# One transfer of 128 rows for each output tile, and another order for the attention of batches 1 and 2, in a global-local attention and gated MLP kernel

## The chip, the cores and the metric

The kernel runs on one core of one Trainium2 chip. The metric is the device time of one execution in microseconds; lower is better.

## The reference

There are 8 batches of 8 heads with head dimension 64. Each batch has 32 global tokens and 512 local ones. The kernel computes attention and puts its output through an MLP (8 x 544 = 4352 tokens, 512 wide, 2048 hidden).

```python
s_g = scale * q_g @ concat(k_g, k_l).T             # global queries see everything
out_g = softmax(s_g) @ concat(v_g, v_l)
s_ll = where(|i - j| <= 32, scale * q_l @ k_l.T, -1e9)   # local queries: a band
s_lg = scale * q_l @ k_g.T                               # and all global keys
out_l = softmax(concat(s_lg, s_ll)) @ concat(v_g, v_l)
x = concat(out_g, out_l) per batch, heads side by side   # (4352, 512)
h = x @ w_in
out = (h * sigmoid(1.702 * h)) @ w_out                   # float32
```

## The kernel before

The order of the instructions on every engine is written out by hand: the tile framework is told to keep the program's order. It adds the semaphore waits.

**Attention.** The unit of work is half a batch, four heads, one for each 32 partitions. `Quad` does batch 0, `Wide` all others; in the text `a` and `c` are the two halves of the batch in work, `a2` the first half of the next. Its methods are the steps:

- `Tk`, `Tq` transpose the loaded keys (`rk`) and queries (`rq`) on VectorE into `kT` and `qt`; `kcopy` and `qcopy` lay some of them out a second time; `transpose_g` does the same for the global queries and keys of a batch (`qgT`, `kgT`), and `ext` copies these beside the local ones. Each copy can run on VectorE or on ScalarE (`on_act`).
- `S(rnd)` computes the scores of one of two rounds on TensorE into a pair of PSUM tiles (`spair`, one buffer each), `X(rnd)` the exponentials on ScalarE, `M(rnd)` the product with the band mask, on VectorE or GpSimd.
- `U(unit)` multiplies the exponentials by ones (unit 0, the sums) and by two halves of the values, `Gm` the same for the global queries. `R` turns the sums into factors on VectorE, `XL(h)` scales into `xL`, the MLP's input; `G` does so for the global rows, into `xG`. `UG` and `RXG` are short for runs of these.

**MLP.** For each batch `h_mm` and `h_act` (together `h_step`) compute one of 16 chunks of the hidden layer for 512 tokens: four matmuls into a bank of PSUM, and a gelu on ScalarE into `gT`. The second product of batches 0 and 1 goes by `o_mm`: sixteen parts of four matmuls, four for each of four tiles of 128 tokens (`osteps` and `o_parts` list them), then `o_out` copies a tile to SBUF on ScalarE and stores it. The second product of later batches goes by `Pair`, with seven products in place of eight (sums of `gT` and of `w_out`, `weight_sums`, are made on VectorE beforehand). The rows of global tokens of all batches, number `B`, form a last block of 256 rows in two tiles.

The banks of PSUM for `hp`, `op`, `ov`, `og`, `px` and `py` come from one pool of four in turn. Exponentials and gelu need different tables in ScalarE; the table is loaded when the function changes, and `exp_table` and `gelu_table` force a load early by an activation of one column.

**Order.** TensorE is kept busy by interleaving: the attention of batch 1 runs among the `osteps` of batch 0, that of batch 2 (and the first half of batch 3) among the `o_parts` of batch 1 in `phase_o1`, later ones in `phase_o`. GpSimd's queue issues the loads of queries, keys, values and weights with a cast to bfloat16, in the order in which they stand between GpSimd's own instructions.

**Stores.** Token t of a tile is not a row of the output in order: within a batch, row `16 r + t` is computed in group t, and a tile has four groups of 32 tokens on 32 partitions each. `tile_out` stores one group after the other:

```python
for j in js:
    rows = out[...].rearrange("(r t) m -> t r m", t=16)[4 * tci + j]   # 32 rows of 512
    eng.dma_start(out=rows, in_=ob[32 * j : 32 * j + 32])
```

SP's queue issues nearly all of them; in the last block GpSimd issues one tile, and ScalarE six quarter pieces. `Pair.store` stores a pair of tiles, `quarter` half the columns of a tile.

Of the kernel before, what the change touches and what calls it, by code (L numbers as in the profile page):

```python
# [20 lines left out]
def kernel(  # L21
# [12 lines left out]
    nc = tc.nc  # L34

    B, H, Sl, D = q_l.shape
    Sg = q_g.shape[2]
    S = Sg + Sl
# [36 lines left out]
    def load(b, us=(0, 1), kq=True):  # L75
        if b not in loaded:
            loaded[b] = (ld.tile([128, 2, 16 * D], BF16, name="rk"),
                         ld.tile([128, 2, 16 * D], BF16, name="rq"))
        if kq:
            s = slice(us[0], us[-1] + 1)  # L80
            nc.gpsimd.dma_start(out=loaded[b][1][:, s], in_=qf[b][:, s])
            nc.gpsimd.dma_start(out=loaded[b][0][:, s], in_=kf[b][:, s])
# [5 lines left out]
    def v_view(b, n):  # L88
        return vtiles[b % 2][:, : 8 * n * (D + 2)].rearrange("p (u j c d) -> p u j c d", u=2, j=4, c=n)
# [16 lines left out]
    def copy_vg1():  # L106
        vt = v_view(1, 5).rearrange("p u j c d -> p (u j) c d")
        src = vt[96:128, :, 0:1, :D]
        on_act(vt[96:128, :, 1:2, :D], src)
        on_act(vt[96:128, :, 3:5, :D], src.to_broadcast([32, 8, 2, D]))  # L110

    def on_act(out_, in_):
        nc.scalar.activation(out_, in_, AF.Copy)  # L113
# [49 lines left out]
    for j in range(4):  # L163
        r = (j + 1) % 4
        nc.gpsimd.memset(bd[32 * r : 32 * r + 32, j, :], 1.0)
    for i in range(2):
# [3 lines left out]
        out=step, in_=step, pattern=[[1, 289]], compare_op=ALU.is_ge,  # L170
# [68 lines left out]
    def transpose_g(lo, hi, names="qk"):  # L239
        for name, dst, s in (("q", qgT, rqg), ("k", kgT, rkg)):  # L240
            if name not in names:
                continue
            nc.vector.transpose(dst[:, lo:hi, :32], s[:, lo:hi].bitcast(F32))
# [39 lines left out]
    def spair():  # L283
        return [psS.tile([128, 2, 512], F32, name="s4", tag="s%d" % i) for i in range(2)]
# [326 lines left out]
    def h_mm(i, fc, hp, kcs):  # L611
        for kc in kcs:
            nc.tensor.matmul(hp[:, : width(i)], lhsT=w_in_c[:, fc // 4, kc, fc % 4 // 2, :, fc % 2],  # L613
                             rhs=(xL[i] if i < B else xG)[:, kc, :],
                             start=(kc == 0), stop=(kc == NKC - 1))
# [7 lines left out]
    def gelu_table():  # L623
        gelu(spot[:, 0:1], spot[:, 1:2])

    def exp_table():
        nc.scalar.activation(spot[:, 0:1], spot[:, 1:2], AF.Exp)
# [5 lines left out]
    def h_step(i, fc):  # L633
        if fc == 0:
            gTs[i] = (moe.tile([128, FC, TB], BF16, name="gT") if i < B else
                      early.bitcast(BF16).rearrange("p a b -> p (a b)").rearrange("p (f t) -> p f t", f=FC))
        hp = pbank("hp")
        h_mm(i, fc, hp, range(NKC))
        h_act(i, fc, hp)

    def o_mm(i, st, out=True):
        tci, f4 = divmod(st, 4)
        first = (i, tci) not in ops
        if first:
            ops[i, tci] = pbank("op")
        op = ops[i, tci]
        for fc in range(4 * f4, 4 * f4 + 4):
            nc.tensor.matmul(op, lhsT=gTs[i][:, fc, tci * 128 : tci * 128 + 128],  # L648
                             rhs=w_out_sb[:, fc, :], start=(first and fc == 4 * f4), stop=(fc == FC - 1))
        if f4 == 3 and out:  # L650
            o_out(i, tci, op)
# [42 lines left out]
    class Pair:  # L694
# [51 lines left out]
        def store(self, engs=(nc.sync, nc.sync)):  # L746
            for h in range(2):
                tile_out(self.i, self.tt + h * (width(self.i) // 256),
                         self.ob[:, 2 * h : 2 * h + 2].rearrange("p h m -> p (h m)"), engs[h])

        def quarter(self, h, m, eng, js=range(4)):
            tile_out(self.i, self.tt + h, self.ob[:, 2 * h + m], eng, slice(m * HM, m * HM + HM), js)

    def tile_out(i, tci, ob, eng=nc.sync, cols=slice(0, d_model), js=range(4)):
        for j in js:
            if i < B:
                rows = out[i * S + Sg : (i + 1) * S, cols].rearrange("(r t) m -> t r m", t=16)[4 * tci + j]
            else:
                r = (4 * tci + j) * S
                rows = out[r : r + Sg, cols]  # L760
            eng.dma_start(out=rows, in_=ob[32 * j : 32 * j + 32])  # L761

    obs = {}

    def o_out(i, tci, op):
        if tci % 2 == 0:
            obs[i, tci // 2] = moe.tile([128, 4, HM], F32, name="ob", bufs=3)
        ob = obs[i, tci // 2][:, tci % 2 * 2 : tci % 2 * 2 + 2].rearrange("p h m -> p (h m)")
        nc.scalar.activation(ob, op, AF.Copy)
        tile_out(i, tci, ob)  # L770

    a, c = Quad(0), Quad(1)
# [81 lines left out]
    def osteps(i, *sts):  # L854
        for tci, f4 in sts:
            o_mm(i, 4 * tci + f4)

    nq = {1: (Wide(2), Wide(3)), 2: (Wide(4), Wide(5))}
    a, c = nq[1]
    copy_vg1()  # L860
    transpose_g(2, 4)
    a.Tk(False)
    a.Tq(False)
    a.ext((0, 1, 2), on_act)
    a.kcopy(on_act)
    a.ext((3,), on_act)
    a.qcopy(on_act)
    osteps(0, (0, 1), (0, 0), (1, 1), (1, 0), (2, 1), (2, 0))
    a.S(0)
    a.X(0)  # L870
    c.Tk()
    c.Tq()
    c.ext()
# [2 lines left out]
    a.S(1)  # L876
    a.X(1)
    a.M(1)
    nq[2][0].Tq(False)
    nq[2][0].Tk(False)  # L880
    osteps(0, (0, 3))
    o_mm(0, 7, False)
    c.S(0)
    c.X(0)
    o_out(0, 1, ops[0, 1])
    c.M(0, nc.gpsimd)
    load(2, (1,))
    load_v(2)
    load(3)
    osteps(0, (2, 3), (3, 0))  # L890
    c.S(1)
    c.X(1)
    nq[2][0].kcopy(on_act)
    nq[2][0].qcopy(on_act)
    for unit in range(3):
        a.U(unit)
    a.R()
# [15 lines left out]
    for kcs in ((0, 1), (2,), (3,)):  # L913
        for fc in range(4):
            h_mm(1, fc, hps[fc], kcs)
    transpose_g(4, 6)
    a.G()
    c.G()
    pt = spair()
    for fc in range(4, 8):  # L920
        h_mm(1, fc, bank(pt, (fc - 2) % 4), range(NKC))

    a, c = nq[2]
# [22 lines left out]
    def o_parts(i, *parts):  # L946
        for part in parts:
            o_mm(i, part)

    def loads_after(i):  # L950
        if i + 2 < B:
            load_v(i + 2)
        if i == 1:
            load_g(8, NQ)
        if i + 3 < B:
            load(i + 3)

    def quads_of(n):
        if n < B and n not in nq:
            nq[n] = (Wide(2 * n), Wide(2 * n + 1))  # L960
        return nq.get(n, (None, None))

    def phase_o1():
        a, c = nq[2]
        a2, c2 = quads_of(3)
        a2.T()
        transpose_g(6, 8)
        a2.ext()
        a.X(0)
        a.M(0)  # L970
        loads_after(1)
        o_parts(1, 0, 1, 2, 3, 4)
        a.S(1)
        a.X(1)
        a.M(1)
        o_parts(1, 5, 6)
        c.S(0)
        c.X(0)
        o_parts(1, 7)
        a.UG()  # L980
        a.R()
        c.M(0)
        c.S(1)
        c.X(1)
        a.XL(0)
        a.XL(1)
        c.M(1)
        a.G()
        o_parts(1, 8, 9)
        a2.S(0)  # L990
        a2.X(0)
        o_parts(1, 10, 11)
        a2.M(0)
        a2.S(1)
        a2.X(1)
        gelu_table()
        c.UG()
        c.RXG()
        a2.M(1)
        o_parts(1, 12, 13, 14, 15)  # L1000

    def phase_o(i):
        b = i + 1
# [69 lines left out]
    for i in range(1, B):  # L1073
        if i > 1:
            for fc in range(FC):
# [3 lines left out]
                if i + 1 < B:  # L1079
                    c = nq[i + 1][1]  # L1080
# [23 lines left out]
    def pair_banks(k):  # L1104
        return [psX.tile([128, 512], F32, name="x", tag="x%d" % (2 * (k % 2) + j)) for j in range(2)]
# [3 lines left out]
    for st in range(FC):  # L1109
        h_step(B, st)  # L1110
        if st < len(todo):
            tt, k = todo[st]
            if k == 3:
                p = Pair(B - 1, tt, pair_banks(tt))
            p.mm(k)
            if k == 4:
                p.m3()
                p.z()
            if k == 6:
                p.zm()  # L1120
            if k == 2:
                p.sub()
                p.evict()
            if k == 7:
                p.add()
                p.store((nc.sync, (nc.sync, nc.gpsimd)[tt]))
        if st in (4, 8, 12):
            g_sums(B, st // 2 - 2, st // 2)
        if st == 14:
            g_sums(B, 6, 7)  # L1130
# [3 lines left out]
    p = Pair(B, 0, (x0, x1, y0, y1))  # L1134
# [14 lines left out]
    p.mm(5)  # L1149
    nc.vector.tensor_sub(zz[0], zz[0], x0[:, :HM])  # L1150
    on_act(p.ob[:, 1], x0[:, :HM])
    p.quarter(0, 1, nc.scalar, (0, 1))
    p.quarter(0, 1, nc.sync, (2, 3))
    p.mm(7)
    nc.vector.tensor_add(p.ob[:, 0], zz[0], y0[:, :HM])
    p.quarter(0, 0, nc.scalar)


# [28 lines left out]
```

## Time and profile before

| | |
|---|---|
| median of 3 runs | 290.76 us (290.74 to 291.71) |
| profiled execution | 293.49 us |
| its span | 291.8 us, mean granted clock of TensorE 0.998 |
| busy share: PE, DVE, ACT, POOL | 96%, 69%, 65%, 38% |
| matmuls | 3727 |
| stores issued: SP, ScalarE, GpSimd | 130, 6, 4 |

The profile is of one execution and is the source of all durations; its own time is 2.7 us above the median, and 1.7 us above its span. PE is TensorE's matmuls, PEld its weight loads, DVE is VectorE, ACT ScalarE, POOL GpSimd, SP the sync engine; a q behind the name is the engine's queue of transfers. A row of the timeline gives start and duration in us, engine, line, operation, output and input, and in brackets how long the engine had been idle and what ended that. Lines are those of the kernel before.

### The profile page before, as it was taken

Reading aid. Unit: us, or ns where it says so; the run is one execution under the profiler, and the core shown is the slowest. Engines: PE = TensorE matmul, PEld = TensorE weight load, DVE = VectorE, ACT = ScalarE, POOL = GpSimd, SP = SyncE. Lnnn points to the kernel's source line nnn. Section 1 sums busy time; section 2 is a strip of 40 time slices with the busy share of each in tenths; the row PEclk is TensorE's granted clock in tenths of the full one; section 3 lists DMA queues with packets and bytes.
Section 4 is the critical chain, followed back from the end, with each engine's and each line's share of the span. In section 5 each row is a group of like instructions: output and inputs, shape, how many; then the busy total and the mean of one; then the engine's idle time right before and its main releaser. Section 6 shows DMA issues by size and latency. Waiting matters only on the chain.

```text
span 291.8 us, 8856 instructions
## 1 busy us (share of the span) xinstructions
PE 280.4 (96%) x3727; PEld 179.0 (61%) x3727; DVE 200.5 (69%) x480; ACT 188.4 (65%) x304; POOL 112.2 (38%) x148
## 2 busy tenths in 40 slices
PE   6899989999999999999899999999999999999993
PEld 6444445444554478646685488646874588458882
DVE  7660157974589899579858898679957697263361
ACT  4847588478686775688458784778658761863431
POOL 8893459976217101790049503760071000000020
PEclk9999999999999999999999999999999999999999
DMA  8999999999959901299025942290112002200222
GB/s 202 157 202 208 203 167 159 161 136 164 166 120 128 151 4 39 58 129 156 6 75 81 149 82 66 55 117 5 28 49 72 2 3 74 72 0 2 72 76 73
DMA packets 59480, 28.24 MB, mean 97 GB/s; under 512 B 47600, under 2 KB 49904, under 8 KB 59440
## 3 DMA queue, kind: packets, MB, share of 16 engines
q0 software_dynamic: 51792, 17.83, 54.8%
q1 hardware_dynamic: 7072, 9.12, 11.3%
q10 hardware_dynamic: 576, 0.72, 0.8%
q8 instruction: 29, 0.48, 0.7%
q14 instruction: 11, 0.09, 0.1%
HBM read 36.31 MB, written 8.91 MB: 155 GB/s over the span
## 4 chain that ended last, share of the span: by engine, by line
PE 80%; DMA 10%; POOL 4%; DVE 2%; issue 1%; ACT 1%; DVEq 0%; POOLq 0%
PE hp L613 34%; PE px L719 12%; PE py L719 9%; PE x L719 6%; PE op L648 6%; PE s L558 5%; DMA rq<-in_q_l_dram 5%; PE ov L584 4%; DMA w_out_sb<-in_moe_w_out_dram 3%; DMA v<-in_v_l_dram 2%; PE s L613 1%; POOL mask L225 1%; POOL w_in_sb L259 1%; DVE xL L469 1%; PE og L595 1%
## 5 line engine op out<-in xcount | busy, mean ns | idle before, releaser
L613 PE MATMUL hp<-xL,w_in_sb 128*128 128x512 bf16 x480 | 105.4, 379 | 0.4 <-DVE xL L469 0.4
L613 PEld LDWEIGHTS <-w_in_sb 128*128 128x128 bf16 x576 | 56.0, 98 | 60.4 <-issue 0.7
L618 ACT ACTIVATE gT<-hp 128x512 bf16<-128x512 f32 x120 | 70.4, 596 | 26.4 <-PE hp L613 24.9
L569 ACT ACTIVATE e<-s 128x1016 bf16<-128x1016 f32 (+1 forms) x56 | 53.3, 1004 | 20.3 <-PE s L558 20.1
L574 POOL TENSOR_TENSOR e<-e,mask 128x1760 bf16<-128x1760 bf16 (+1 forms) x9 | 29.6, 3290 | 76.1 <-ACT e L569 76.1
L719 PEld LDWEIGHTS <-gs 128*128 128x128 bf16 x480 | 46.2, 98 | 6.3
L692 DVE TENSOR_TENSOR gs<-gT 128x512 bf16<-128x512 bf16 (+1 forms) x90 | 30.4, 365 | 18.8 <-ACT gT L618 18.7
L98 POOL DMA_DIRECT2D v<-in_v_l_dram x40 | 31.3, 791 | 15.9 <-PE og L595 12.1
L719 PE MATMUL py<-wsum,gs 128*128 128x256 bf16 x240 | 30.3, 273 | 0.0
L648 PE MATMUL op<-w_out_sb,gT 128*128 128x512 bf16 x128 | 29.5, 380 | 0.2 <-DMA w_out_sb<-in_moe_w_out_dram 0.2
L761 POOL DMA_DIRECT2D out_dram<-ob x4 | 2.1, 534 | 61.3 <-ACT early L618 61.3
L574 DVE TENSOR_TENSOR e<-e,mask 128x1712 bf16<-128x1712 bf16 (+1 forms) x19 | 21.0, 1104 | 5.2 <-ACT e L569 5.2
L510 DVE STREAM_TRANSPOSE kT<-rk 128x512 f32<-128x512 f32 x14 | 14.6, 1045 | 9.5 <-DMA rk<-in_k_l_dram 9.5
L648 PEld LDWEIGHTS <-gT 128*128 128x128 bf16 x128 | 11.9, 98 | 14.1 <-issue 0.2
L719 PEld LDWEIGHTS <-gT 128*128 128x128 bf16 x192 | 18.0, 98 | 2.8
L719 PE MATMUL px<-w_out_sb,gT 128*128 128x256 bf16 x160 | 19.2, 273 | 0.0
L719 PE MATMUL px<-w_out_sb,gs 128*128 128x256 bf16 x160 | 19.1, 273 | 0.0
L558 PEld LDWEIGHTS <-kT 32*128 32x128 bf16 x672 | 13.0, 93 | 9.2 <-issue 6.4
L469 DVE TENSOR_TENSOR xL<-ov,rs 128x512 bf16<-128x512 f32 x27 | 17.9, 687 | 0.9 <-PE ov L436 0.4
L689 DVE TENSOR_TENSOR gs<-gT 128x1024 bf16<-128x1024 bf16 (+1 forms) x30 | 17.4, 580 | 0.0
L558 PE MATMUL s<-q,kT 32*128 32x160 bf16 (+1 forms) x448 | 15.4, 246 | 1.5 <-issue 1.0
L113 ACT ACTIVATE ob<-px 128x512 f32<-128x512 f32 x10 | 6.0, 597 | 15.0 <-DVE zz L741 15.0
(149 smaller groups left out, 361.2 us busy)
## 6 DMA issues: line engine op xcount, KB each, us to landing
out_dram<-ob SPq DMA_DIRECT2D x128, 64.0 KB, 1.8
rq<-in_q_l_dram POOLq DMA_DIRECT2D x5, 512.0 KB, 6.4
rk<-in_k_l_dram POOLq DMA_DIRECT2D x5, 512.0 KB, 8.2
v<-in_v_l_dram POOLq DMA_DIRECT2D x24, 96.0 KB, 4.0
w_in_sb<-in_moe_w_in_dram POOLq DMA_DIRECT2D x8, 256.0 KB, 7.7
w_out_sb<-in_moe_w_out_dram POOLq DMA_DIRECT2D x4, 512.0 KB, 10.8
rq<-in_q_l_dram POOLq DMA_DIRECT2D x5, 256.0 KB, 6.2
rk<-in_k_l_dram POOLq DMA_DIRECT2D x5, 256.0 KB, 6.2
```

The lines of the kernel that those rows point to most:

```text
L98: nc.gpsimd.dma_start(out=vt[0:n, hs, c, :D], in_=vs[FIRST[c] : FIRST[c] + n, hs])
L469: nc.vector.tensor_mul(self.x[:, 2 * self.u + h, :], self.st[1 + h], self.st["rs"])
L510: nc.vector.transpose(flat[:, 0:Sl].rearrange("p (r t) -> p t r", t=16), loaded[self.b][0][:, self.u].bitcast(F32))
L558: nc.tensor.matmul(bank(self.ps, j)[:, at : at + n], lhsT=self.k[p, KEYS[c] : KEYS[c] + 128, e], rhs=qs[p, :, :, e], start=(e == 0), stop= ...
L569: nc.scalar.activation(self.E[rnd][:, 2 * i : 2 * i + 2, :n], self.ps[i][:, :, :n], AF.Exp, scale=scale)
L574: eng.tensor_mul(e, e, mask[:, rnd : rnd + 1, :n].to_broadcast([128, 4, n]))
L613: nc.tensor.matmul(hp[:, : width(i)], lhsT=w_in_c[:, fc // 4, kc, fc % 4 // 2, :, fc % 2], rhs=(xL[i] if i < B else xG)[:, kc, :], start=( ...
L618: nc.scalar.activation(out_, in_, AF.Gelu_apprx_sigmoid)
L648: nc.tensor.matmul(op, lhsT=gTs[i][:, fc, tci * 128 : tci * 128 + 128], rhs=w_out_sb[:, fc, :], start=(first and fc == 4 * f4), stop=(fc = ...
L689: nc.vector.tensor_tensor(sums[i][2][:, g, :n], t[:, g, 0, :n], t[:, g, 1, :n], ALU.add)
L692: nc.vector.tensor_tensor(sums[i][k][:, g, : n // 2], x[:, g], y[:, g], op)
L719: nc.tensor.matmul(out_, lhsT=lv[:, g, tt * 128 : tt * 128 + 128], rhs=rv[:, g, :], start=(g == 0 and k in ((1, 3, 4, 6) if self.apart els ...
```

## The change

`tile_out` stores the groups that it is given by one transfer: 128 partitions of `ob` to a pattern of 4 x 32 rows of the output. The tail's stores are dealt to the queues anew: a pair's second tile of the last batch goes by SP and no longer by GpSimd, the first quarter whole by SP, the last one in two halves by ScalarE and SP. In the built program 140 stores become 36: on SP 33 of 4 x 32 x 512 elements, one of 4 x 32 x 256 and one of 2 x 32 x 256, on ScalarE one of 2 x 32 x 256.

For batch 1's attention, the exponentials' table is loaded right behind batch 0's last gelu; `kcopy`, `qcopy` and two of four `ext` copies run on VectorE in place of ScalarE; `transpose_g` stands behind the half's own transposes; `copy_vg1` (copies of the global values on ScalarE) stands behind the first exponentials; the second half's first mask product is VectorE's and not GpSimd's. The transposes of batch 2's first half (`nq[2][0]`) move from the middle of this stage to its end, behind `G`, with their copies on VectorE, ahead of `transpose_g(4, 6)`. In `phase_o1` the parts of batch 1's second product are dealt differently among the attention's rounds, and `a.G`, `c.UG`, `c.R`, `c.XL` and `c.G` stand at other places. The number of matmuls is the same.

```diff
@@ -752,13 +752,12 @@
             tile_out(self.i, self.tt + h, self.ob[:, 2 * h + m], eng, slice(m * HM, m * HM + HM), js)
 
     def tile_out(i, tci, ob, eng=nc.sync, cols=slice(0, d_model), js=range(4)):
-        for j in js:
-            if i < B:
-                rows = out[i * S + Sg : (i + 1) * S, cols].rearrange("(r t) m -> t r m", t=16)[4 * tci + j]
-            else:
-                r = (4 * tci + j) * S
-                rows = out[r : r + Sg, cols]
-            eng.dma_start(out=rows, in_=ob[32 * j : 32 * j + 32])
+        j0, j1 = js[0], js[-1] + 1
+        if i < B:
+            rows = out[i * S + Sg : (i + 1) * S, cols].rearrange("(r t) m -> t r m", t=16)[4 * tci + j0 : 4 * tci + j1]
+        else:
+            rows = out[:, cols].rearrange("(b s) m -> b s m", s=S)[4 * tci + j0 : 4 * tci + j1, :Sg]
+        eng.dma_start(out=rows, in_=ob[32 * j0 : 32 * j1])
 
     obs = {}
 
@@ -857,17 +856,16 @@
 
     nq = {1: (Wide(2), Wide(3)), 2: (Wide(4), Wide(5))}
     a, c = nq[1]
-    copy_vg1()
+    exp_table()
+    a.Tk()
+    a.Tq()
     transpose_g(2, 4)
-    a.Tk(False)
-    a.Tq(False)
-    a.ext((0, 1, 2), on_act)
-    a.kcopy(on_act)
-    a.ext((3,), on_act)
-    a.qcopy(on_act)
+    a.ext((0, 1), on_act)
+    a.ext((2, 3))
     osteps(0, (0, 1), (0, 0), (1, 1), (1, 0), (2, 1), (2, 0))
     a.S(0)
     a.X(0)
+    copy_vg1()
     c.Tk()
     c.Tq()
     c.ext()
@@ -876,22 +874,18 @@
     a.S(1)
     a.X(1)
     a.M(1)
-    nq[2][0].Tq(False)
-    nq[2][0].Tk(False)
     osteps(0, (0, 3))
     o_mm(0, 7, False)
     c.S(0)
     c.X(0)
     o_out(0, 1, ops[0, 1])
-    c.M(0, nc.gpsimd)
+    c.M(0)
     load(2, (1,))
     load_v(2)
     load(3)
     osteps(0, (2, 3), (3, 0))
     c.S(1)
     c.X(1)
-    nq[2][0].kcopy(on_act)
-    nq[2][0].qcopy(on_act)
     for unit in range(3):
         a.U(unit)
     a.R()
@@ -913,9 +907,11 @@
     for kcs in ((0, 1), (2,), (3,)):
         for fc in range(4):
             h_mm(1, fc, hps[fc], kcs)
-    transpose_g(4, 6)
     a.G()
     c.G()
+    nq[2][0].Tk()
+    nq[2][0].Tq()
+    transpose_g(4, 6)
     pt = spair()
     for fc in range(4, 8):
         h_mm(1, fc, bank(pt, (fc - 2) % 4), range(NKC))
@@ -973,31 +969,34 @@
         a.S(1)
         a.X(1)
         a.M(1)
-        o_parts(1, 5, 6)
+        o_parts(1, 5, 6, 7)
         c.S(0)
         c.X(0)
-        o_parts(1, 7)
         a.UG()
         a.R()
         c.M(0)
+        o_parts(1, 8)
         c.S(1)
         c.X(1)
         a.XL(0)
         a.XL(1)
+        a.G()
         c.M(1)
-        a.G()
-        o_parts(1, 8, 9)
+        o_parts(1, 9, 10, 11)
         a2.S(0)
         a2.X(0)
-        o_parts(1, 10, 11)
+        c.UG()
+        c.R()
         a2.M(0)
+        c.XL(0)
+        c.XL(1)
+        o_parts(1, 12)
         a2.S(1)
         a2.X(1)
         gelu_table()
-        c.UG()
-        c.RXG()
+        c.G()
         a2.M(1)
-        o_parts(1, 12, 13, 14, 15)
+        o_parts(1, 13, 14, 15)
 
     def phase_o(i):
         b = i + 1
@@ -1123,7 +1122,7 @@
                 p.evict()
             if k == 7:
                 p.add()
-                p.store((nc.sync, (nc.sync, nc.gpsimd)[tt]))
+                p.store()
         if st in (4, 8, 12):
             g_sums(B, st // 2 - 2, st // 2)
         if st == 14:
@@ -1149,11 +1148,11 @@
     p.mm(5)
     nc.vector.tensor_sub(zz[0], zz[0], x0[:, :HM])
     on_act(p.ob[:, 1], x0[:, :HM])
-    p.quarter(0, 1, nc.scalar, (0, 1))
-    p.quarter(0, 1, nc.sync, (2, 3))
+    p.quarter(0, 1, nc.sync)
     p.mm(7)
     nc.vector.tensor_add(p.ob[:, 0], zz[0], y0[:, :HM])
-    p.quarter(0, 0, nc.scalar)
+    p.quarter(0, 0, nc.scalar, (0, 1))
+    p.quarter(0, 0, nc.sync, (2, 3))
 
 
 # ---- launch: one core; inputs and outputs as the reference has them ----
```

## The prediction

> **What bounds the kernel now.** I read the page, then the chain of waits, then the timeline engine by engine where the change falls, and last the DMA queues. From the page:
>
> ```profile
> PE 280.4 (96%) x3727; PEld 179.0 (61%) x3727; DVE 200.5 (69%) x480; ACT 188.4 (65%) x304; POOL 112.2 (38%) x148
> PE   6899989999999999999899999999999999999993
> DMA  8999999999959901299025942290112002200222
> q1 hardware_dynamic: 7072, 9.12, 11.3%
> q10 hardware_dynamic: 576, 0.72, 0.8%
> out_dram<-ob SPq DMA_DIRECT2D x128, 64.0 KB, 1.8
> ```
>
> TensorE is busy from slice 5 (about 33 us) to the end, so only its waits and the tail can be won. The transfers are busy in nearly every slice until 80 us, then mostly idle. The timeline of PE from 36 to 92 us has these waits worth naming:
>
> ```profile
> 38.28 0.53 PE L558 MATMUL s<-q,kT 32*128 32x160 bf16 x16 [0.55 <-ACT kT L113]
> ...
> 42.74 1.89 PE L648 MATMUL op<-w_out_sb,gT 128*128 128x512 bf16 x8 [0.19 <-DMA w_out_sb<-in_moe_w_out_dram]
> ...
> 55.87 1.89 PE L613 MATMUL hp<-xL,w_in_sb 128*128 128x512 bf16 x8 [0.45 <-DVE xL L469]
> ...
> 78.81 0.34 PE L595 MATMUL og<-v,e 128*32 128x66 bf16 x20 [0.36 <-ACT ob L769]
> ```
>
> With a 0.15 us wait at 52.1 that is 1.7 us in all. VectorE in the same stretch:
>
> ```profile
> 50.04 2.13 DVE L574 TENSOR_TENSOR e<-e,mask 128x1712 bf16<-128x1712 bf16 x1
> ...
> 69.38 1.04 DVE L510 STREAM_TRANSPOSE kT<-rk 128x512 f32<-128x512 f32 x1 [5.58 <-DMA rk<-in_k_l_dram]
> ```
>
> A mask product takes 2.13 us, not the 1.05 of its like, while GpSimd runs one of its own (3.37 us from 47.88); and VectorE stands 5.58 us for the keys of batch 3. The tail:
>
> ```profile
> 280.76 8.61 SPq L761 DMA_DIRECT2D out_dram<-ob  x10
> ...
> 286.77 2.77 ACTq L761 DMA_DIRECT2D out_dram<-ob  x6
> 286.77 0.42 DVE L1155 TENSOR_TENSOR ob<-zz,x 128x256 f32<-128x256 f32 x1 [0.45 <-PE x L719]
> ```
>
> The last arithmetic ends at 287.19, the span at 291.8. In between ScalarE's queue issues six stores one after the other until 289.54, and the last store has landed at 290.33.
>
> **The stores, tail first.** 140 stores of 32 rows become 36; the four that GpSimd issued (free, after 61 us of idling) go to SP: one issue behind the other tile's at 280.8, and SP is idle after that until 285.9. Issuing: a 32-row store holds its queue 0.31 to 0.46 us. A 128-row one in the new form is not in the trace; the 128-row loads of SP and ACT hold theirs 0.43 to 0.47, four old stores 1.8. I take 0.5. The last issue then starts at 287.3 (SP: last quarter's second half, behind the quarter issued at 286.77) where it started at 289.10: 1.8 us earlier, about 1.5 at the end of the data.
>
> Moving the data is the disputed cost. Queue q1 carried 134 transfers (128 + 2 stores, 4 loads); their rows are 128 x 32 + 2 x 32 + 2 x 128 + 2 x 256 = 4,928 packets, and 7,072 - 4,928 = 2,144 = 134 x 16. So each transfer ended with a post from all 16 DMA engines, two rows on each for a store. All of them had a leading dimension of 32 or 128 on both sides. The new store has 128 partitions on one side and, in the built program, 4 x 32 rows of 2 KB on the other (the interleaved rows of four groups can't be one dimension); the halves of the last quarter have 64 and 2 x 32. No row shows how such a pattern is dealt. Bounds: over 16 engines (8 rows each), or in equal shares of both leading dimensions, as every transfer of the trace is: then 4 shares at most, 32 rows each, and 2 for the halves. I take the second, since 4 can't be cut 16 ways while 32 and 128 can.
>
> [...]
>
> Price: by the trace's packet records a 2 KB packet alone on its engine takes 0.084 to 0.087 us, a 1 KB one 0.044 to 0.047. An upper bound is the answer on the queues from 268 to 280 us, eight stores alone:
>
> ```profile
> q1 hardware_dynamic: 384, 0.52, 17.1%
> ```
>
> 256 data packets and 128 posts took 17.1% of 16 engines' 12 us, 32.8 us: 0.128 each, with overlaps counted twice. I take 0.085 and 0.045. So 32 rows in line are 2.7 us (1.44 for 1 KB rows) where two rows were 0.17. Data starts about 1 us after an issue starts. On the busiest engine: two tiles of the last batch, issued from 280.8, run 281.8 to 287.25; the global tile (issued 285.94) to 289.97; the quarter to 291.4; the two halves, if they share that engine, to 294.3. Against 290.33 that is **+4.0 us**. If the halves use different engines, +2.5.
>
> **The stores earlier.** Behind 80 us nothing waits for a store: an output buffer is written again three pairs later and the transfers stand idle. Between 44 and 62 us they don't: batch 0's four tiles put 4 x 2.7 = 10.9 us on four engines in place of 2.7 on each, so loads queued there are late by up to 8.2 us. Against it stands that GpSimd no longer does the mask product ahead of the loads of batches 2 and 3, which are issued up to 3.3 us sooner (1.3, where the engines are full anyway). Keys of batch 3, landed at 69.37, would come 4.9 to 6.9 us later at worst. VectorE stands in `a2.T` for them, and behind it the masks of batch 2: 2.9 us of transposes and copies, then 1.07 and 1.05, which TensorE needs by 77.2. That leaves 2.8 us of slack, so 0 to 3.7 us (nothing if the queues interleave better than in line). I take **+1.5**.
>
> **Batch 1 laid out anew.** Copies go from ACT to DVE and the exp table is loaded ahead of them: gelu is done at 33.19 and ACT then stood 2.08 us for `v_g`, which covers the load of 1.28. `copy_vg1` (1.57 us on ACT) goes behind the first exponentials, from 40.4 to 42.0, where the second scores are ready at 41.96; without that cover it would cost what it ran over. Keys land at 34.54; transposes and copies on DVE end near 37.3, ACT's two extensions near 37.55; TensorE arrives at 37.73, so the 0.55 is gone. It is given back: four groups later TensorE waits for the last part of `w_out_sb`, which lands at 42.70 as before, and 0.19 becomes 0.74. Net 0. Then the mask product of c leaves GpSimd for DVE (47.2 to 48.3, DVE idle there), the next takes 1.05, `xL` comes 0.6 earlier, and of 0.15 + 0.45 about 0.13 is left: **-0.47**.
>
> The transposes of batch 2's queries and keys (`nq[2][0]`, 2.2 us with copies) now stand on DVE ahead of `transpose_g(4, 6)`, whose result the `ext` copies on ACT wait for; before it came at 56.33, now near 59.5. Queued behind the first of these copies on ACT are the gelus of chunks 1 to 7. By their old spacing (57.64 to 61.89 without the wait) the pair that frees the score banks ends at 63.8, and TensorE comes to `a.S(0)` at 63.1: **+0.7**. It was free before, and is free again if DVE is 0.7 earlier.
>
> In `phase_o1` part 7 moves ahead of `c.S(0)`, so the ACT copy that frees the `og` bank runs before the exponentials instead of after: **-0.36**. `c.UG` comes with its mask ready by about 0.1 us; if not, some tenths. `exp` there stays covered by three parts (2.6 us). Sum of this half: -0.47 + 0.7 - 0.36 = **-0.1**, with ends at -0.9 (no wait at `a.S(0)`) and +1.
>
> **Sum.** 4.0 + 1.5 - 0.1 = +5.4. The profiled execution took 293.49 (span 291.8 and 1.7 around it), the median 290.76; as times added or removed I put it on the median: 296.2, and near 298.9 for a profiled one.
>
> **Rivals.** (1) It ends faster: the 128 partitions are dealt over 16 engines whatever the other side leads with. For it: the SBUF side is whole, and q1 never used fewer. Then the tail gains 1.5, no load is late, and 290.76 - 1.5 - 0.1 = 289.1 (288.4 to 290.5). It decides from the point where a store's posts come from more than 8 engines. [...] (2) Four engines, but the halves part and no load is late: 290.76 + 2.5 - 0.1 = 293.2; against it, both halves have the same shape. (3) Four engines at 0.128 us a packet: the tail chain from 281.8 becomes 3 x 4.1 + 3 x 2.05 = 18.4, to 300.2, +9.9: 302 with late loads. Against it, overlaps inflate that price.
>
> **How the numbers follow.** Forecast, four engines in line: 0.70, its own range 294.7 (no late load) to 298.4 (3.7 us of it). Rival 1: 0.17. Rival 2: 0.08. Rival 3: 0.05. A measurement of this kernel tells 0.5%, 1.45 us, from no change: the bounds are 289.3 and 292.2. Slower: 0.70 + 0.05 + 0.05 = 0.80 with part of rival 2; faster 0.10 (over half of rival 1), the same 0.10. A range that leaves out no more than 2 in 10 must take in most of rival 1: 289.0 to 299.0.
>
> **What would show it.** Right: q1 has 5,386 packets (4,416 rows stored, 768 loaded, 64 posts of loads, 34 x 4 + 2 of stores; 16 posts a store would make it 5,808); stores land in 3 us and more instead of 1.8; the tail after the last arithmetic is near 8.6 us instead of 4.6; PE waits about 0.7 us at 42.7 for `w_out_sb` and again before 64 for ACT, not at 38.3, 55.9 or 78.8. The keys of batch 3 land after 72 us, and PE waits near 77 for DVE. Wrong: 5,808 packets, landing under 2 us, and a tail near 3 us; then the time is 289.

## The result, and the profile after

The kernel after took 300.87 us (median of 4 runs, 300.56 to 301.78), the kernel before 291.04 us beside it (290.74 to 291.71): a ratio of 1.034 with a 95% interval of 1.031 to 1.037, so 9.8 us slower where 5.4 had been forecast, and above the forecast range of 289.0 to 299.0. The direction was right; two terms of the sum were not.

From the page of the kernel after, the lines that answer to those shown of before:

```profile
PE 278.2 (93%) x3704; PEld 178.9 (60%) x3727; DVE 201.9 (68%) x487; ACT 186.4 (62%) x299; POOL 106.7 (36%) x143
PE   6999998899899999999999999999999999999930
DMA  7999999959999901197518972590210012001121
q1 hardware_dynamic: 5386, 9.50, 10.7%
q10 hardware_dynamic: 354, 0.59, 0.6%
```

q1 carries 5,386 packets, the number worked out for four engines a store (two a half). (The trace lacks 23 records of matmuls; the weight loads are 3,727 as before.) The 40th slice of PE is empty and the 39th a third full: the tail. Slices 7, 8 and 11 hold new waits. The timeline of PE there, behind one earlier row:

```profile
43.64 0.53 PE L558 MATMUL s<-q,kT 32*128 32x160 bf16 x14 [0.32 <-ACT e L569]
...
52.57 0.21 PE L595 MATMUL s<-v,e 96*32 96x66 bf16 x4 [1.32 <-DMA v<-in_v_l_dram]
...
54.35 0.35 PE L584 MATMUL s<-e,v 128*32 128x72 bf16 x9 [0.62 <-issue]
...
78.02 0.38 PE L584 MATMUL ov<-e,ones 128*32 128x128 bf16 x12 [0.50 <-DVE e L574]
78.97 0.35 PE L584 MATMUL ov<-e,ones 128*32 128x72 bf16 x12 [0.58 <-DVE e L574]
```

TensorE waits 0.32 us for exponentials, which it did not before. The values of batch 1 are late (1.32 us), then comes a wait with no releaser ("issue", 0.62), then two for mask products. The mask products are late because VectorE stood for the keys of batch 3, as the timeline of VectorE shows:

```profile
73.99 1.05 DVE L510 STREAM_TRANSPOSE kT<-rk 128x512 f32<-128x512 f32 x1 [8.18 <-DMA rk<-in_k_l_dram]
...
76.89 2.03 DVE L574 TENSOR_TENSOR e<-e,mask 128x1760 bf16<-128x1760 bf16 x2
```

And the tail, SP's and ScalarE's queues and VectorE's last instruction:

```profile
280.85 7.16 SPq L760 DMA_DIRECT2D out_dram<-ob  x5
...
286.86 0.42 DVE L1153 TENSOR_TENSOR ob<-zz,x 128x256 f32<-128x256 f32 x1 [0.45 <-PE x L719]
287.31 1.13 ACTq L760 DMA_DIRECT2D out_dram<-ob  x1
```

The arithmetic ends at 287.28 and the issues at 288.4; by the packet records the last data of a store ends at 296.72, and the span at 298.77. The data are the tail now, not the issues.

The first profile of before was of an untypical execution (293.49 us against a median of 290.76), so the kernel before was profiled once more, as the first experiment. Against that second profile the loss is laid out so:

| us | before, second profile | after | difference |
|---|---|---|---|
| last arithmetic ends | 284.98 | 287.28 | +2.30 |
| from there to the last data | 3.20 | 9.44 | +6.24 |
| from there to the end of the span | 1.44 | 2.05 | +0.61 |
| span | 289.62 | 298.77 | +9.15 |

The tail is 11.49 us instead of 4.64, +6.9 where +4.0 was forecast. The middle is +2.3 here, and 9.8 - 6.9 = 2.9 by the medians, where 1.5 - 0.1 = 1.4 was forecast.

### The profile page after: what moved, and what is told of

Same layout as the page of the kernel before. It is cut to its first block, busy times and chain, and to the rows that moved or that the text cites. A ratio compares the mean times of both kernels' runs of the same rounds, so it can differ in the third digit from the quotient of the medians.

```text
span 298.8 us, 8653 instructions
## 1 busy us (share of the span) xinstructions
PE 278.2 (93%) x3704; PEld 178.9 (60%) x3727; DVE 201.9 (68%) x487; ACT 186.4 (62%) x299; POOL 106.7 (36%) x143
## 3 DMA queue, kind: packets, MB, share of 16 engines
q1 hardware_dynamic: 5386, 9.50, 10.7%
## 4 chain that ended last, share of the span: by engine, by line
PE 69%; DMA 16%; POOL 9%; DVE 2%; issue 1%; POOLq 0%
PE hp L613 30%; PE px L719 12%; PE py L719 9%; PE x L719 6%; DMA v<-in_v_g_dram 6%; PE ov L584 5%; DMA rq<-in_q_l_dram 4%; PE s L558 4%; DMA w_out_sb<-in_moe_w_out_dram 3%; DMA rk<-in_k_l_dram 3%; PE op L648 2%; POOL w_in_sb L259 2%; POOL v L98 2%; POOL v L249 1%; POOL mask L225 1%
## 5 line engine op out<-in xcount | busy, mean ns | idle before, releaser
L613 PE MATMUL hp<-xL,w_in_sb 128*128 128x512 bf16 x465 | 104.3, 379 | 0.9 <-issue 0.2
L574 POOL TENSOR_TENSOR e<-e,mask 128x1760 bf16<-128x1760 bf16 (+1 forms) x8 | 26.2, 3281 | 56.9 <-ACT e L569 56.9
L648 PE MATMUL op<-w_out_sb,gT 128*128 128x512 bf16 x122 | 28.9, 380 | 0.5 <-issue 0.3
L574 DVE TENSOR_TENSOR e<-e,mask 128x1760 bf16<-128x1760 bf16 (+1 forms) x20 | 20.8, 1045 | 5.3 <-ACT e L569 5.2
L100 POOL DMA_DIRECT2D v<-in_v_g_dram x24 | 14.1, 589 | 23.8 <-DMA v<-in_v_g_dram 12.6
```

The costliest lines, as they stand in the source:

```text
L574: eng.tensor_mul(e, e, mask[:, rnd : rnd + 1, :n].to_broadcast([128, 4, n]))
```

## The experiments

**The kernel before, once more.** No edit.

> The kernel before, unchanged, profiled a second time. Theory (the first profile was of an untypical execution, 2.7 us above the kernel's own median, with the last part of w_out_sb landing at 42.70 us): a second profiled execution takes 290 to 292 us, w_out_sb lands before 41 us and TensorE reaches the later stages 1 to 3 us earlier than in the first profile, with the same tail of 4.6 us. Rival (profiling itself costs it 2.7 us): 293 to 294 us again, with the same waits.

Measured: 291.32 us, span 289.6; the last part of `w_out_sb` landed at 41.65, later than expected but 1.05 ahead of the first profile, TensorE was 1.0 us ahead at the `h_mm` matmuls near 55 us and 2.2 at the end. The theory holds: the first profile had a late transfer of weights, and a wait of 0.96 us without a releaser that ends at 141.41 and that this one lacks. A profile's spread of 2 us is as large as the terms in question, so the profile to compare with is one whose time lies at the median.

**The layout alone.** The kernel after with the old loop in `tile_out` and the old dealing of the tail to queues.

```diff
-        eng.dma_start(out=rows, in_=ob[32 * j0 : 32 * j1])
+        for j in js:
...
+            eng.dma_start(out=rows, in_=ob[32 * j : 32 * j + 32])
...
-                p.store()
+                p.store((nc.sync, (nc.sync, nc.gpsimd)[tt]))
...
```

> The kernel after with every store as in the kernel before (32 rows each, the last quarters dealt as before), so only the new layout of batches 0 and 1 is left. Theory (stores are nearly all of the loss, layout costs nothing): 290.0 to 291.5 us against 291.0; keys of batch 3 land before 71 us. Rival (the layout carries the 2.8 us that the tail of 7.0 leaves over): 293 to 294 us.

Measured: 293.53 us against 291.33, ratio 1.0072 (1.0046 to 1.0098): +2.2 us. The rival has it: the new layout, priced at -0.1, costs about 2. The timeline of PE in this kernel names the place:

```profile
51.59 0.76 PE L584 MATMUL s<-e,v 128*32 128x128 bf16 x39
54.55 0.35 PE L584 MATMUL s<-e,v 128*32 128x72 bf16 x9 [2.19 <-issue]
```

TensorE stops inside a run of 72 matmuls (`c.U`) whose inputs are all there. The wait has no releaser, but the packet records show one packet of 16 KB on the instruction queue from 52.14 to 53.10, and TensorE goes on 1.45 us behind it. That this packet carries TensorE's instructions is worked out from counts (the last section); it is called TensorE's fetch from here on. The queues from 51.5 to 54 us:

```profile
q0 software_dynamic: 1514, 0.24, 130.6%
q1 hardware_dynamic: 208, 0.29, 34.8%
q8 instruction: 1, 0.02, 2.4%
```

In these 2.5 us the packets of q0, GpSimd's loads, take 130.6% of the engines' time and those of q1 34.8% (overlaps count twice), and the one instruction packet runs among them. In the second profile of before the same packet started at 48.77, 3.4 us sooner. GpSimd's timeline, first of that profile of before, then of this kernel, shows what else had moved:

```profile
46.83 3.38 POOL L574 TENSOR_TENSOR e<-e,mask 128x1760 bf16<-128x1760 bf16 x1
50.13 0.62 POOL L81 DMA_DIRECT2D rq<-in_q_l_dram  x1
```

```profile
46.31 0.56 POOL L81 DMA_DIRECT2D rq<-in_q_l_dram  x1 [0.31 <-DMA rk<-in_k_l_dram]
```

Without the mask product (`c.M(0)`) in front, the loads of batches 2 and 3 are issued 3.8 us sooner. That they push the fetch back became the theory of the later experiments.

**The stores alone.** The kernel before with `tile_out` and the dealing of the tail as in the kernel after.

```diff
-        for j in js:
...
-            eng.dma_start(out=rows, in_=ob[32 * j : 32 * j + 32])
+        j0, j1 = js[0], js[-1] + 1
...
+        eng.dma_start(out=rows, in_=ob[32 * j0 : 32 * j1])
...
```

> The kernel before with the new stores alone (one transfer of 128 rows, last quarters dealt as in the kernel after). Theory (tail +7, late loads +2 to +3): 299 to 301.5 us, tail after the last arithmetic 11.5 us. Rival (the layout carries 2.8 us): 297.5 to 298.5 us.

Measured: 299.81 us, ratio 1.031 (1.026 to 1.036): +8.5. The last arithmetic ends at 285.99, 1.0 later than in the second profile of before, and the tail is 11.47 us as in the kernel after. So the whole excess of the tail belongs to the stores, and the early stores cost 1.0 by the profile or 8.5 - 6.9 = 1.6 by the medians. PE's timeline has the largest piece of that:

```profile
52.23 0.21 PE L595 MATMUL s<-v,e 96*32 96x66 bf16 x4 [1.06 <-DMA v<-in_v_l_dram]
```

Nothing like the wait of 2.19 us without a releaser is here: GpSimd has its mask product, the loads go out from 49.60, and the instruction fetch starts at 48.52.

**The tail undone.** The kernel after with the old loop, here `tile_out4`, for batch 7 and the global tokens, and the old dealing of the tail.

```diff
...
     def tile_out(i, tci, ob, eng=nc.sync, cols=slice(0, d_model), js=range(4)):
+        if i >= B - 1:
+            return tile_out4(i, tci, ob, eng, cols, js)
...
```

> The kernel after with 32-row stores for the last batch's tiles and for the global tokens only, the last quarters dealt as before: the tail is undone, the early stores stay. Theory (late loads cost 2 to 3 us by themselves): 293 to 294.5 us, tail 4.6 us, keys of batch 3 still landing after 73 us. Rival (all of the loss is the tail): 290.5 to 291.5 us.

Measured: 295.50 us, ratio 1.0144 (1.0115 to 1.0173): +4.2, 1 us above the theory's range. The tail is back at 5.39 us (0.75 of it a longer way from the last data to the end), and the rival, that all of the loss is the tail, is out. Between the layout alone and this kernel lie 2.0 us, of which 5.39 - 4.60 = 0.8 is in the tail; 1.2 is left for the early stores. The profile has TensorE waiting 1.92 us for the values of batch 1, this row and 0.19 behind it:

```profile
52.98 0.21 PE L595 MATMUL s<-v,e 96*32 96x66 bf16 x4 [1.73 <-DMA v<-in_v_l_dram]
```

**The early stores undone.** The kernel after with the old loop for batches 0 and 1 alone.

```diff
...
     def tile_out(i, tci, ob, eng=nc.sync, cols=slice(0, d_model), js=range(4)):
+        if i < 2:
+            return tile_out4(i, tci, ob, eng, cols, js)
```

> The kernel after with 32-row stores for batches 0 and 1 only; the other stores and the tail stay as in the kernel after. Theory (the early stores cost about 2.0 us, as the difference of e3 and e1 says, the tail 6.9): 298.5 to 299.5 us against 300.9 for the kernel after; values of batch 1 no longer keep TensorE near 52 us, and the tail after the last arithmetic stays 11.5 us. Rival (the loss in the middle comes from the layout alone): 300.5 to 301 us.

Measured: 300.43 us, ratio 1.032 (1.028 to 1.035), only 0.4 below the kernel after: the theory's 2.0 is refuted as a sum of parts. In the profiled execution the last arithmetic ends at 286.83, 0.45 sooner than in the kernel after; its tail is 12.33 us where 11.5 was expected, with 39 slow packets (over 0.12 us) in place of 29, for which no run gives a reason. TensorE no longer waits for the values of batch 1 (1.32 us in the kernel after), but the wait without a releaser, 0.62 us there, grows:

```profile
54.76 0.35 PE L584 MATMUL s<-e,v 128*32 128x72 bf16 x9 [2.27 <-issue]
```

The fetch starts at 52.49. Late values and a late fetch fall on the same stretch: with the one gone, TensorE waits for the other, 2.27 us in place of 1.32 and 0.62. So 2.1 (layout) and 1.0 to 1.6 (early stores) together make 2.9, not 3.1 to 3.7.

**Loads late again, by the mask product.** The layout alone, with one word given back.

```diff
-    c.M(0)
+    c.M(0, nc.gpsimd)
```

> The kernel e1 (new layout, old stores) with the mask product of c given back to GpSimd, ahead of the loads of batches 2 and 3, which are then issued about 3.5 us later. Theory (the layout's 2.1 us come from these loads being issued sooner: TensorE's instruction fetch lands behind them, TensorE stands 2.2 us near 52 us and its granted clock falls to 0.8): the fetch starts before 50 us, no stand, clock 1.0 there, 290.5 to 291.7 us. Rival (the loss lies in the new order on VectorE and ScalarE): 293 to 294 us.

Measured: 291.95 us, ratio 1.0038 (1.0008 to 1.0068): by the medians 1.6 us of the 2.2 are gone, by the ratios 1.0; 291.95 lies just above the theory's range. The execution that was profiled took 294.63 us, with a late `w_out_sb` like that of the first profile of before:

```profile
44.53 1.89 PE L648 MATMUL op<-w_out_sb,gT 128*128 128x512 bf16 x8 [2.07 <-DMA w_out_sb<-in_moe_w_out_dram]
```

In it the fetch started at 51.43, not before 50 as expected, but TensorE itself was late and did not stand near 52 us. Counted by TensorE's weight loads, of which no record is missing, the packet was on time: it started at the 623rd, where in the two profiles of before it started at the 624th and 625th, and in that of the layout alone at the 734th.

**Loads late again, by time alone.** The layout alone, with GpSimd kept busy.

```diff
     c.M(0)
+    for _ in range(17):
+        nc.gpsimd.memset(v_view(2, 5)[:, :, :, :, D:], 1.0)
     load(2, (1,))
```

> The kernel e1 with GpSimd filling the same ones of the values' tile 17 more times (about 3.5 us) ahead of the loads of batches 2 and 3; the mask product stays on VectorE, so only the time of the loads changes. Theory (the early loads delay TensorE's instruction fetch): 290.3 to 291.5 us, fetch before 50 us, no stand near 52 us. Rival (the mask product on VectorE, or the new order of copies, costs the 2.1 us): 293 to 294 us.

Measured: 291.22 us against 291.40, ratio 0.9998 (0.9975 to 1.0020). The loads go out at 50.17, the fetch starts at 48.82 (the 622nd weight load), and TensorE doesn't stand near 52 us. (The profiled execution took 292.79 us, the longest of its ten; it has a wait of 1.22 us of the same kind at 140.68.) The layout's loss is gone with nothing changed but when the loads start. The table by stretches from 51 to 63 us, first of the layout alone, then of this kernel (the columns are busy time of PE, PEld, DVE, ACT and POOL, then the granted clock, the share of the DMA engines, overlaps counted twice, and GB/s):

```profile
51.00:57.00 6.00, 3.59 (x117) 2.16 (x115) 4.12 (x11) 0.60 (x1) 4.14 (x7) 0.82 1.84 202
57.00:63.00 6.00, 6.00 (x27) 2.58 (x26) 5.90 (x11) 3.41 (x7) 5.13 (x8) 0.90 1.29 217
```

```profile
51.00:57.00 6.00, 5.91 (x133) 3.23 (x132) 5.34 (x14) 1.49 (x2) 5.69 (x10) 1.00 1.16 175
57.00:63.00 6.00, 5.72 (x27) 2.49 (x26) 5.93 (x10) 5.01 (x11) 3.95 (x7) 1.00 1.67 133
```

The profile of the layout alone loses time twice: TensorE is 2.19 us without work, and behind that, at a granted clock of 0.82 and 0.90, the run of `h_mm` matmuls took 11.34 us (54.83 to 66.17) instead of 9.92 (52.80 to 62.72). Of these 3.6 us 2.3 are left at the last arithmetic (287.24, against 284.98 in the second profile of before); where the rest is won back was not followed.

**The one edit alone.** The kernel before with the mask product on VectorE.

```diff
-    c.M(0, nc.gpsimd)
+    c.M(0)
```

> The kernel before with one edit: the mask product of c goes from GpSimd to VectorE, so that the loads of batches 2 and 3, queued behind it on GpSimd, are issued about 3.4 us sooner. Theory (these early loads delay TensorE's instruction fetch and are the layout's whole cost): 293 to 294 us, the fetch after 51 us and TensorE standing 1.5 to 3 us near 53 us. Rival (another part of the layout is needed for the loss): 290.5 to 291.4 us, a little faster since VectorE's own product no longer takes 2.13 us.

Measured: 292.93 us against 290.77, ratio 1.0088 (1.0053 to 1.0123): +2.2 us from one word, as much as the whole layout. The profiled execution (291.80 us, the shortest of its six) has the fetch start at 50.81, the 655th weight load, and this line in PE's timeline, a somewhat shorter stand than expected:

```profile
53.39 0.35 PE L584 MATMUL s<-e,v 128*32 128x72 bf16 x10 [1.29 <-issue]
```

Taking the mask product off GpSimd does make VectorE's own shorter (1.01 us, where the second profile of before has 1.84), but it costs more than it brings.

**Stores to successive rows.** The kernel after; the destination leads with 128 (64 for the halves). The permutation of the output rows is left out, and the tiles of global tokens go to rows of batch 7.

```diff
...
+        r = min(i, B - 1) * S + Sg + 128 * (tci if i < B else 2 + tci)
+        rows = out[r + 32 * j0 : r + 32 * j1, cols]
```

> The kernel after with each store of 128 rows going to 128 successive rows of the output (64 for the halves), so that its destination leads with 128 or 64 instead of 4 or 2; the permutation of the output rows is left out. Theory (the leading 4 is the cause): posts from 16 engines, 5,808 packets on q1, tail of about 3 us after the last arithmetic, no late values or keys; the layout's 2.1 us stay: 290.5 to 293 us. Rival (one large transfer is slow whatever its shape): 5,808 packets or not, a tail of 9 us and more, 298 to 301 us.

Measured: 294.81 us, ratio 1.0118 (1.0093 to 1.0142). q1 has 5,808 packets, 16 posts a store; the tail is 4.10 us, its last data 1.97 us behind the arithmetic, against 9.44. So the size of a transfer is not at fault, the 128 rows are the same; the leading 4 is. The total is 1.8 us above the theory's range. In the profile TensorE stood 2.97 us without a releaser (the fetch started at 53.49), the granted clock was 0.85 from 51 to 57 us, and the last arithmetic ended at 288.37, 1.1 later than in the layout alone.

**Eight groups instead of four, and four groups of successive rows.** The kernel after with other rows for the tiles of batches, the permutation left out; `g` is 8 in one run, as here, and 4 in the other.

```diff
-            rows = out[i * S + Sg : (i + 1) * S, cols].rearrange("(r t) m -> t r m", t=16)[4 * tci + j0 : 4 * tci + j1]
+            rows = out[i * S + Sg + 256 * (tci // 2) : i * S + Sg + 256 * (tci // 2 + 1), cols].rearrange("(g h r) m -> h g r m", g=8, h=2)[tci % 2]
```

> The kernel after with the tiles of batches stored to 8 groups of 16 successive rows of the output (the permutation is left out), so that the destination leads with 8 instead of 4; the global tokens are stored as in the kernel after. Theory (engines are dealt by the leading dimension, and each of few engines loses time at the start of a store): 8 posts a store, q1 at 5,386 + 32 x 4 = 5,514 packets, a lone pair of stores lands in 3 to 4.5 us (2.6 in line on 8 engines, with a start of 0.5 to 2) between the 7.2 of four engines and the 1.5 of sixteen. Rival (the slow start comes from rows 32 KB apart, and these rows are successive): 2.6 us. Time 297 to 300 us.

> The kernel after with the tiles of batches stored to 4 groups of 32 successive rows (the permutation is left out): the destination still leads with 4, but the rows that one engine writes are successive instead of 32 KB apart. Theory (the slow start belongs to 32 rows in line on one engine): a lone pair of stores takes 7.2 us as in the kernel after, the tail stays 11.5 us, 300 to 301 us. Rival (the slow start comes from rows 32 KB apart): a lone pair takes 5.1 us (64 x 0.080), the tail is near 9.5 us, 298 to 299 us.

Measured: 300.15 and 301.59 us, one run each, 0.2 and 0.6 above what was expected. With 8 groups q1 has 5,514 packets, as worked out. From 272 to 280 us two stores of 256 KB run alone; the DMA row and q1 of that stretch (a digit is 0.2 us), of the kernel after, of the 8 groups and of the 128 successive rows:

```profile
DMA  0002520421012221222222222222226222221100
q1 hardware_dynamic: 264, 0.52, 21.6%
```

```profile
DMA  0000567243355455555553100000000040000000
q1 hardware_dynamic: 272, 0.52, 22.5%
```

```profile
DMA  0000001899999700000000000000000000000002
q1 hardware_dynamic: 288, 0.52, 17.3%
```

The digits are tenths of 16 engines' time, and the packets beyond the 256 rows, 8, 16 and 32 for the two stores, are the posts: a 2 with 4 posts a store, a 5 with 8, a 9 with 16. Equal bytes, and the length of the row is the time. The records name no engine, but in the kernel after 4 packets run at once for 5.2 of the 7.19 us. By the packet records:

| engines | in line (packets x 0.080 us) | measured | more |
|---|---|---|---|
| 4 | 64: 5.1 us | 7.19 us | 2.1 |
| 8 | 32: 2.6 us | 3.81 us | 1.2 |
| 16 | 16: 1.3 us | 1.51 us | 0.2 |

The time beyond the line is in slow packets, most of them in the first two microseconds: on four engines 20 of the 256 take 0.14 to 0.94 us, on eight 38 take 0.12 to 0.50, on sixteen none takes more than 0.11. The zeros and ones at the start of the first row are these. With 4 groups of successive rows the pair takes 7.19 us as well, and the tail's burst 14.71 us against 14.69, so rows 32 KB apart are not the cause. Why a long line on few engines starts slowly stays open; no run tells it.

**The old tail over three queues.** The kernel before.

```diff
-    p.quarter(0, 1, nc.scalar, (0, 1))
-    p.quarter(0, 1, nc.sync, (2, 3))
+    p.quarter(0, 1, nc.scalar, (0,))
+    p.quarter(0, 1, nc.sync, (1,))
+    p.quarter(0, 1, nc.gpsimd, (2, 3))
...
-    p.quarter(0, 0, nc.scalar)
+    p.quarter(0, 0, nc.scalar, (0, 1))
+    p.quarter(0, 0, nc.sync, (2, 3))
```

> The kernel before with its last eight stores dealt over three queues: of the first quarter one each to ScalarE's and SP's queue and two to GpSimd's, of the last quarter two each to ScalarE's and SP's. Theory (the tail after the last arithmetic is the line of issues on ScalarE's queue, 2.8 us for six): the last issue starts 1.0 to 1.4 us earlier, tail 3.4 to 3.7 us instead of 4.6, 290.0 to 290.5 us against 291.4. Rival (the end of the data, not the issue, sets the tail): no change, 291.4 us.

Measured: 290.89 us against 290.77, ratio 1.0001 (0.9981 to 1.0021): no gain. The queues:

```profile
277.92 8.40 SPq L761 DMA_DIRECT2D out_dram<-ob  x11
...
283.93 1.36 ACTq L761 DMA_DIRECT2D out_dram<-ob  x3
```

ScalarE's issues now end at 285.29, but SP has four stores of the global tile in front and starts its last one at 285.84, 1.5 us behind the arithmetic, where the old tail's last was 2.0 behind. Half a microsecond less at the issue became 0.4 at the data (2.77 behind the arithmetic instead of 3.20), and the way to the end of the span took 0.3 of it back. No version tried beats the kernel before.

## Why the prediction was right or wrong

**Four engines: right.** The packets came out as worked out, and with them the posts, 4 a store (q1 has 202 packets of 4 bytes: 64 of the loads, 34 x 4 + 2 of the stores); the runs with 8 and 16 posts extend it: 5,386, 5,514 and 5,808 packets. That a store is dealt by the leading dimension was the author's choice between two bounds. The runs bear it out for the dimensions that they have: 2, 4 and 8 gave 2, 4 and 8 posts, 32, 64 and 128 gave 16. That all stores fall on the same four engines, which the line in the sum rests on, no run shows, since the records name no engine; what they show in its place is 4 packets at once in 3.7 of the 4.5 us from 284.5 to 289.0 in the kernel after, with the stores issued at 280.85, 281.44 and 286.02 under way, where two stores side by side on engines of their own would add up to 8. The issue of a 128-row store held SP's queue 0.54 us (0.71 in two cases) against 0.5 assumed.

**The tail, +4.0: mis-sized, +6.9.** The step that failed is "32 rows in line are 2.7 us": it counts a store on one engine by the price of its packets and puts nothing for a slow start. In line the packets are even cheaper than assumed: 0.080 us for 2 KB and 0.042 for 1 KB, so the chain of 96 + 96 packets is 11.7 us, not 12.5. But the burst runs from 282.03 to 296.72, 14.7 us: 3 us are lost. About 2 of them, by an estimate, are slow packets: 29 of the 640 take more than 0.12 us, together 8 us longer than the others' 0.084, on four engines. A price taken from stores of two rows per engine can't show that. Another 0.6 lies behind the last data. The halves do share engines, as taken: 2 packets at once in 2.3 of the 3.0 us from 293.6 to 296.6, not 4. Rival 3's total of 302 is near the measured one, but its price of 0.128 a packet isn't found; the time is lost at the starts.

**The early stores, +1.5: about right in size, in part by luck.** 1.0 to 1.6 by the runs. The path that the forecast prices is there: in the kernel after the keys of batch 3 landed at 73.97 (after 72, as said) and VectorE passed it on to the masks, 1.08 us on TensorE. But with the stores alone this path cost only 0.43 us, and the values of batch 1, not in the forecast, 1.06 (1.32 in the kernel after). The forecast's range has a slip besides: 6.9 us of delay less 2.8 of slack are 4.1, not 3.7.

**The layout, -0.1: wrong, +2.1.** The step that failed is "the mask product of c leaves GpSimd", booked as -0.47, together with "issued up to 3.3 us sooner", booked as relief for late loads. The loads did go out that much sooner, and TensorE's fetch came behind them (at 52.14 in the layout alone, at 48.82 with the loads late again), which the sum has at nothing: the prediction looks at the queues of SP, ScalarE and GpSimd but not at TensorE's own. The rest of the layout came out near its -0.1: with the loads late again it measured 0, within 0.7 us. In the profile of that run the waits at 55.87 and 78.81 (0.45 and 0.36 us) are gone, and the `a.S(0)` wait for ScalarE, forecast at 0.7, is 0.58:

```profile
63.29 0.54 PE L558 MATMUL s<-q,kT 32*128 32x160 bf16 x16 [0.58 <-ACT gT L618]
```

In the kernel after it is hidden since TensorE comes later. A wait of 0.32 us for exponentials (at 43.64 in the kernel after) was not in the forecast: `copy_vg1` ran from 40.10 to 41.67 and the second exponentials came behind it, a cover that the prediction took to suffice. That the 0.55 at 38.28 is gone shows nothing, since the second profile of before lacks it too. The forecast 0.74 for `w_out_sb` came from an untypical landing at 42.70 (41.65 in the second profile of before); in the kernel after it landed at 40.15 and nothing waited.

**Rival 1** is what the run with successive rows shows, with 0.5 us less tail than before, not 1.5: the data ended 1.2 us sooner, 0.7 of which was lost behind them.

## What to carry to other kernels

Before joining small stores into one, look at what both access patterns lead with: two transfers that led with 4 moved their rows on 4 engines in 7.2 us where 16 engines took 1.5, and at the end of this kernel the tail grew by 6.9 us. When an edit lets transfers start sooner in a stretch where the DMA engines are full (q0 alone took 130.6% of their time in the layout alone, overlaps counted twice), list what else is queued there, TensorE's instruction packets included: a wait "issue" inside a run of ready matmuls, with a packet on the instruction queue just before its end, was such a delay here (2.19 us, ended 1.45 us behind the packet, and gone with the loads issued 3.9 us later). And take the profile that a sum starts from at the kernel's median time.

## What the runs showed of the hardware that was not expected

The profile has a queue of instruction packets, 29 of 16 KB, and loads of data that were issued early held the one near 50 us up: it started at 52.14 with these loads from 46.31 on (the layout alone), and at 48.82 with the loads from 50.17 on, and nothing else changed. The page of before has the queue:

```profile
q8 instruction: 29, 0.48, 0.7%
```

That the packets are TensorE's instructions is worked out, not recorded: 29 packets for 7,454 matmuls and weight loads are one for some 257, and TensorE's waits follow them. In all 14 profiles TensorE has 13 waits of 0.4 us and more without a releaser, and each ends 1.2 to 1.6 us after such a packet has landed; the 0.96 us of the first profile of before is one of them. The fifth packet is the one near 50 us. In the five profiles where it started at 48.3 to 50.0, and in that of the layout with the mask product given back, this was at TensorE's 622nd to 625th weight load, 0.3 to 1.0 us after the 620th, and TensorE did not stand near 52 us. In the other eight, all with early loads, it started 2.7 to 4.9 us after the 620th. TensorE stood for it in five of them (50.81 to 53.49), always behind its 734th weight load; in the other three the waits for values of batch 1, 0.8 to 1.9 us, covered the delay.

The granted clock in the stretch from 51 to 57 us fell to 0.82 and 0.85 after two of these waits (2.19 and 2.97 us), and to 0.77 after the 1.92 us for values in the run with the tail undone; it stayed at 1.00 after 2.27 us in the run with the early stores undone. So the clock fell after some of these waits and not by their length; no run tells what decides.

From the last data to the end of the span it took 1.44 and 1.46 us in the profiles of before, and 2.05 in that of after, where GpSimd issues no stores at the end: its clearing of semaphores and what follows it took 0.89 us instead of 0.45. The run with the tail undone has 2.19 with GpSimd's stores in place and 0.45 for the clearing, so this is not the only cause; no run tells the others.
